# Probability transposes as 64-row halves in two PSUM banks, both heads together, in a block-causal attention and gated MLP kernel

## The chip, the cores and the metric

The kernel runs on one core of a Trainium2 chip. The core has a matrix engine, TensorE (PE in the profile; its weight loads stand apart as PEld), and three other compute engines: VectorE (DVE), ScalarE (ACT) and GpSimd (POOL). SyncE (SP) issues the DMAs here. Matmul results land in PSUM, which this kernel uses as eight banks of 512 fp32 columns for each of the 128 partitions. The metric is the device time of one execution in microseconds (us), as the median over runs; lower is better.

## The reference

Attention with a block-causal mask (blocks of 64), over 8 batches of 8 heads, 576 positions and 64 columns a head, then a gated MLP in which the gate mixes positions:

```python
scores = scale * np.matmul(q, k.transpose(0, 1, 3, 2))
mask = block_i >= block_j
scores = np.where(mask, scores, -1000000000.0)
scores = scores - np.max(scores, axis=-1, keepdims=True)
attn = np.exp(scores)
attn = attn / (np.sum(attn, axis=-1, keepdims=True) + 1e-09)
x = np.matmul(attn, v)            # heads side by side: (8, 576, 512)
...
h = np.maximum(x @ w_in, 0.0)     # 1024 columns
u, v = (h[..., :d_ff // 2], h[..., d_ff // 2:])
v_n = (v - mu) / np.sqrt(var + 1e-06)
v_s = np.einsum('ts,bsd->btd', w_spatial, v_n) + b_spatial[None, :, None]
return (u * v_s) @ w_out
```

The inputs are fp32, save the weights w_in and w_out, which come as 64-bit floats and are narrowed on the chip.

## The kernel before

**Tiling.** Heads go in pairs: 4 pairs a batch, 32 in all. The queries and keys of a pair lie on 128 partitions, 64 for each head. A pair has seven slots, `SLOTS`, each a tile of probabilities `p` of 128 query rows by up to 576 key columns: slots 0 and 1 hold query blocks 0 and 1 of the first and second head (128 + 256 columns), slots 2 and 3 block 2 (384 columns), slots 4 and 5 block 3 (512 columns), and slot 6 the last 64 queries of both heads, one head on each half of the partitions (576 columns).

**The steps of a slot.** `scores` (L265) and `scores_last` (L277) make the products on TensorE; after the first batch each is three products of a high and a low part. The score matmuls of L265 contract 64 rows, one head on each half of the array, and the profile shows them as 64*128. `exps` takes the negated maximum on DVE (L296, L305) and the exponential on ACT (L312). `norm` adds a small number and inverts the sum on DVE (L321, L324) and scales `p` on POOL (L326). `transposes` turns `p` so that keys lie on partitions (L352, L366): the tile of p is the loaded operand and the identity the moving one. The result is copied from PSUM (L354, L356, L361, L367) into `ptlo` (query blocks 0 and 1), `pthi` (blocks 2, 3 and the last queries) and `c4` (the last 64 keys). When all seven slots are there, `av` multiplies by the values (`avl` L396, `avh` L405) and `x_evac` (L382, L383) takes the result out in a high and a low part.

**PSUM.** Four banks serve the scores (`ps_s`), two the transposes and the `av` results together (`ps_t`), and two the MLP (`ps_m`). In `transposes` each slot takes one bank, slot 6 a second one for its last 64 keys.

**The MLP.** `moe` returns 29 groups for a finished batch, each some 8 to 24 matmuls in one bank: `mv` (L436, L447), `mu` (L505), `ms` (L528, L532, L533) and `mo` (L549). These are called expert matmuls below. They wait in `queue` and are dealt out over the 28 slots of the next batch.

**Order.** One loop runs over all slots, and in step n it emits, in this order: at slot 0 the scores of slots 0 to 3, the load of the next values and the background work that splits operands; `norm` of slot n-1; at slot 2 the scores of slots 4 and 5 and the `av` of the pair before; at slot 5 the last scores; `transposes` of slot n-2; about one MLP group; and `exps` of slot n. So on TensorE the transposes of slot 5 stand behind the scores of the next pair, those of slot 0 behind `av`, those of slot 3 behind `scores_last`, and the others between MLP groups. The compiler's scheduler may move single instructions from this order where it takes an operand to be late.

Of the kernel before, what the change touches and what calls it, by code (L numbers as in the profile page):

```python
# [10 lines left out]
F32 = mybir.dt.float32  # L11
# [6 lines left out]
P = 128  # L18
S = 576
# [9 lines left out]
SLOTS = [(0, 0, 1), (1, 0, 1), (0, 2, 2), (1, 2, 2), (0, 3, 3), (1, 3, 3), (2, 4, 4)]  # L29
NS = len(SLOTS)  # L30
# [6 lines left out]
def kernel(  # L37
# [10 lines left out]
    nc = tc.nc  # L48
# [8 lines left out]
    FULL = S // P  # L57

    const = ctx.enter_context(tc.tile_pool(name="const", bufs=1))
# [4 lines left out]
    pt_p = ctx.enter_context(tc.tile_pool(name="pt_p", bufs=1))  # L64
# [5 lines left out]
    ps_t = ctx.enter_context(tc.tile_pool(name="ps_t", bufs=2, space=PSUM))  # L70
# [5 lines left out]
    ident = const.tile([P, P], F32, name="ident")  # L76
# [21 lines left out]
    vs_b = const.tile([P, DH], F32R, name="vs_b")  # L98
    nc.gpsimd.memset(vs_b[64:97, :].bitcast(F32), 1.0)
    nc.gpsimd.memset(ws_b[64:97, :].bitcast(F32), 0.0)  # L100
    c4 = const.tile([P, P], F32, name="c4")
    nc.gpsimd.memset(c4[64:P, :], 0.0)

    staged = []

# [94 lines left out]
    def load_pair(b, pr):  # L200
        if b == 0 and pr % 2:
            raw = ff_p.tile([P, ND, S], F32, tag="u", name=f"raw_{b}_{pr}")
            raw = raw.rearrange("p c t -> p (c t)")[:, :KQ]
        else:
            raw = raw_p.tile([P, KQ], F32, tag="raw", name=f"raw_{b}_{pr}")
        if b == 0 and pr == 0:
            for cs in (slice(0, 256), slice(S, S + 256), slice(256, S), slice(S + 256, KQ)):
                nc.sync.dma_start(raw[:, cs], qk[b, pr, :, cs])
        else:
            nc.sync.dma_start(raw, qk[b, pr])  # L210
        raws[(b, pr)] = raw

    def prep_pair(b, pr):

        raw = raws.pop((b, pr))
        hi = hl_p.tile([P, KQ], F32R, tag="hi", name=f"hi_{b}_{pr}")
        lo = hl_p.tile([P, KQ], F32R, tag="lo", name=f"lo_{b}_{pr}")
        split_of[(b, pr)] = (hi, lo)
        for cs in (slice(0, S), slice(S, KQ)):
            nc.scalar.copy(hi[:, cs], raw[:, cs])  # L220
            yield
        for n, cs in enumerate((slice(S, Q8), slice(0, HT), slice(HT, S), slice(Q8, KQ))):
            (nc.vector if n == 0 else nc.gpsimd).tensor_tensor(  # L223
                out=lo[:, cs], in0=raw[:, cs], in1=hi[:, cs].bitcast(F32), op=ALU.subtract
            )
            yield
# [3 lines left out]
    def load_v(b, pr):  # L230
        vt = v_p.tile([P, FULL + 1, P], F32, tag="v", name=f"v_{b}_{pr}")
        nc.sync.dma_start(vt, v[b, pr])
        vts[(b, pr)] = vt
# [18 lines left out]
    def scores(b, pr, slots):  # L252

        parts = operands(b, pr)
        for i in slots:
            banks[(b, pr, i)] = s_bank(b, f"{b}_{pr}_{i}", slots[0] == 4)
        for i in slots[::2]:
            o = 0
            for t in range(SLOTS[i][1], SLOTS[i][2] + 1):
                n = P * (t + 1)  # L260
                qs = slice(S + t * P, S + (t + 1) * P)
                for m, (a, k) in enumerate(parts):
                    for hd in range(2):
                        js = slice(64 * hd, 64 * hd + 64)
                        nc.tensor.matmul(  # L265
                            banks[(b, pr, i + hd)][:, o:o + n], a[js, qs], k[js, :n],
                            start=(m == 0), stop=(m == len(parts) - 1),
                        )
                o += n
# [12 lines left out]
    ptiles = {}  # L282
# [50 lines left out]
    def pt_tiles(b, pr):  # L333
        if (b, pr) not in pts:
            lo = pt_p.tile([P, 2, 384], F32, tag="ptlo", name=f"ptlo_{b}_{pr}")
            hi = pt_p.tile([P, 2, 4, 320], F32, tag="pthi", name=f"pthi_{b}_{pr}")
            pts[(b, pr)] = (lo, hi)
        return pts[(b, pr)]

    def transposes(b, pr, i):  # L340
        hd, t0, t = SLOTS[i]
        pt = ptiles.pop((b, pr, i))[0]
        lo, hi = pt_tiles(b, pr)

        def bank(tag):
            return ps_t.tile([P, 512], F32, tag="t", name=f"t_{b}_{pr}_{tag}")

        bk = bank(i)
        n = 3 if t == 1 else min(t + 1, 4)

        for c in range(n):
            nc.tensor.transpose(bk[:, c * P:(c + 1) * P], pt[:, c * P:(c + 1) * P], ident)  # L352
        if t == 1:
            (nc.scalar.copy if b == 0 else nc.vector.tensor_copy)(lo[:, hd, :], bk[:, 0:384])  # L354
        elif hd < 2:
            nc.scalar.copy(  # L356
                hi[:, hd, 0:n, (t - 2) * P:(t - 1) * P],
                bk[:, :n * P].rearrange("p (c q) -> p c q", q=P),
            )
        else:  # L360
            nc.scalar.copy(  # L361
                hi[:, :, :, 256:320].rearrange("p h c q -> p c h q"),
                bk.rearrange("p (c h q) -> p c h q", c=4, h=2),
            )
            bk = bank(f"{i}c4")
            nc.tensor.transpose(bk[0:64, 0:P], pt[:, 4 * P:S], ident)  # L366
            nc.scalar.copy(c4[0:64, :], bk[0:64, 0:P])  # L367

    xts = {}
    tails = {}  # L370
# [8 lines left out]
    def x_evac(b, pr, av, q0, n):  # L379
        x = x_tiles(b, pr)  # L380
        qs = slice(q0, q0 + n)
        nc.scalar.copy(x[:, 0, qs], av[:, :n])  # L382
        nc.vector.tensor_tensor(  # L383
            out=x[:, 1, qs], in0=av[:, :n], in1=x[:, 0, qs].bitcast(F32), op=ALU.subtract
        )

    def av(b, pr):

        lo, hi = pts.pop((b, pr))
        vt = vts.pop((b, pr))  # L390
        al = ps_t.tile([P, 512], F32, tag="t", name=f"avl_{b}_{pr}")
        ah = ps_t.tile([P, 512], F32, tag="t", name=f"avh_{b}_{pr}")
        for c in range(2):
            for j in range(2):
                js = slice(64 * j, 64 * j + 64)
                nc.tensor.matmul(  # L396
                    al[js, c * P:256], vt[:, c, js],
                    lo[:, j, 0:256] if c == 0 else lo[:, j, 256:384],
                    start=(c == 0), stop=(c == 1),
                )  # L400
        for c in range(5):
            for j in range(2):
                js = slice(64 * j, 64 * j + 64)
                q0 = (0, 0, 0, 128, 256)[c]
                nc.tensor.matmul(  # L405
                    ah[js, q0:320], vt[:, c, js], hi[:, j, c, q0:] if c < 4 else c4[:, js],
                    start=(c == 0), stop=(c == 4),
                )
        x_evac(b, pr, al, 0, 256)
        x_evac(b, pr, ah, 256, 320)  # L410
        x = xts[(b, pr)]

        nc.gpsimd.tensor_scalar(
            out=tails[b][:, pr], in0=x[:, :, FULL * P:].bitcast(F32), scalar1=1.0, scalar2=1.0,
            op0=ALU.mult, op1=ALU.mult,
        )
# [166 lines left out]
    def spread(gen, n, first, last):  # L583
        background.append([gen, n / (last - first), first, 0.0])
# [22 lines left out]
    def at(n):  # L607

        g, i = divmod(n, NS)
        return (*pairs[g], i) if 0 <= g < len(pairs) else None  # L610

    for n in range(N + 2 * NS):
        g, i = divmod(n, NS)
        here = pairs[g] if g < len(pairs) else None
        if here and i == 0:
            scores(*here, (0, 1, 2, 3))
        if here and g + 1 < len(pairs):
            b, pr = pairs[g + 1]
            if i == 0:
                load_v(b, pr)  # L620
                if g + 1 >= NPAIR:
                    load_pair(b, pr)
            if n == 0:
                load_pair(0, 1)
            if i == LAST + 1 and g + 2 < NPAIR:
                load_pair(0, g + 2)
            if i == 1 and b > 0:
                spread(prep_pair(b, pr), 7, n, n + 4)
        step_background(n)
        if at(n - 1):  # L630
            norm(*at(n - 1))
        if i == RUN2:
            if here:
                scores(*here, (4, 5))
            if 0 < g <= len(pairs):
                av(*pairs[g - 1])
                if g % NPAIR == 0:
                    gs = moe(pairs[g - 1][0])
                    queue += gs
                    rate = len(gs) / (NPAIR * NS)  # L640
        if here and i == LAST:
            scores_last(*here)
        if n >= 2 and at(n - 2):
            transposes(*at(n - 2))
        credit += rate
        while credit >= 1.0 and queue:
            queue.pop(0)()
            credit -= 1.0
        if at(n):
            exps(*at(n))  # L650
# [47 lines left out]
```

## Time and profile before

| what | value |
|---|---|
| time, median of 3 runs | 767.68 us (765.17 to 773.61) |
| span of the profiled execution, first to last instruction | 763.8 us |
| busy TensorE | 740.3 us (97%), 5508 matmuls |
| busy weight loads | 636.0 us (83%) |
| busy DVE, ACT, POOL | 471.9, 436.1 and 318.4 us |
| mean granted TensorE clock | 0.996 |

The span is given for the profiled execution alone; its time beside the span is not recorded. A row of the timeline reads: start in us from the span's start, length in us from the first instruction's start to the last one's end, engine, line, operation, output <- inputs, tile of the array (rows*columns), moving operand, how many instructions are merged; in brackets the engine's idle time before and what ended it. A row of a group has, behind the bar, busy us and mean ns of one instruction, then the idle time of the engine before such instructions. A matmul's length holds its way through the array, so matmuls overlap; the step from one start to the next tells what one costs in a stream. In a row of the waits stand the total in us, the number of waits and, last, the longest.

### The profile page before, as it was taken

To read this page: it belongs to the slowest core of one execution; us is meant where nothing else is said; L and a number is where in the kernel's file an instruction comes from. 1 tells how busy PE (TensorE), PEld (TensorE's weight loads), DVE (VectorE), ACT (ScalarE), POOL (GpSimd) and SP (SyncE) were. 2 spreads that over 40 slices of the span, in tenths; PEclk is the share of its full clock that TensorE was granted. 3 is DMA by queue.
4 is the path that set the end of the run, shared out by engine and by line. 5 is a ranking of instruction groups with operands and counts; after the bars stand their busy time and mean duration, and the time that the engine had idled before them with its cause. 6 is when DMAs were issued, how large, how long until landed. Compare 5 with 4: busy or idle time off the path is not lost.

```text
span 763.8 us, 15854 instructions
## 1 busy us (share of the span) xinstructions
PE 740.3 (97%) x5508; PEld 636.0 (83%) x5508; DVE 471.9 (62%) x1743; ACT 436.1 (57%) x1236; POOL 318.4 (42%) x480
## 2 busy tenths in 40 slices
PE   8998889999999999999999999999999999999998
PEld 5556678987998878898888888898789987889898
DVE  6985984548745577547764577455874557742641
ACT  6885665656665556654655656564666555653232
POOL 4786465423444334442344423542344433431011
PEclk9999999999999999999999999999999999999999
DMA  6453231221122111221012211122112211000001
GB/s 215 151 170 103 84 98 33 75 82 34 52 69 72 42 51 51 69 71 58 18 51 82 78 38 50 30 71 84 33 52 73 67 42 51 18 33 32 1 9 55
DMA packets 21411, 48.63 MB, mean 64 GB/s; under 512 B 2386, under 2 KB 11090, under 8 KB 21332
## 3 DMA queue, kind: packets, MB, share of 16 engines
q1 hardware_dynamic: 21332, 47.63, 19.7%
q8 instruction: 44, 0.72, 0.4%
q14 instruction: 35, 0.29, 0.1%
HBM read 38.18 MB, written 9.44 MB: 62 GB/s over the span
## 4 chain that ended last, share of the span: by engine, by line
PE 81%; DVE 8%; ACT 5%; POOL 2%; issue 2%; DMA 1%; SPq 0%; ACTq 0%; DVEq 0%; POOLq 0%
PE mo L549 14%; PE ms L528 13%; PE mu L505 10%; PE t L352 10%; PE mv L436 10%; PE s L265 7%; PE avh L405 6%; PE s L277 3%; PE avl L396 2%; ACT p L312 2%; PE mv L447 1%; DVE st L457 1%; POOL p L326 1%; PE ms L533 1%; PE ms L532 1%
## 5 line engine op out<-in xcount | busy, mean ns | idle before, releaser
L326 POOL TENSOR_SCALAR p<-p,ssum 128x128 f32<-128x128 f32 (+4 forms) x288 | 177.9, 630 | 209.9 <-DVE ssum L324 173.9
L312 ACT ACTIVATE p<-p,nmax 128x128 f32<-128x128 f32 (+4 forms) x288 | 166.9, 581 | 59.6 <-DVE nmax L296 47.3
L296 DVE CUSTOM_DVE_ANT_0 p<-s,mask 128x128 f32<-128x128 f32 (+3 forms) x256 | 115.4, 484 | 62.8 <-PE s L265 62.7
L352 PE MATMUL t<-ident,p 128*128 128x128 f32 x768 | 124.6, 278 | 10.5 <-POOL p L326 7.2
L505 PE MATMUL mu<-x,wi_hi 128*128 128x288 f32 x512 | 116.5, 304 | 0.6 <-DVE vr L453 0.5
L352 PEld LDWEIGHTS t<-ident,p 128*128 128x128 f32 x768 | 90.6, 141 | 27.8 <-POOL p L326 12.3
L223 POOL TENSOR_TENSOR lo<-raw,hi 128x288 fp32r<-128x288 f32 (+1 forms) x84 | 66.9, 815 | 80.8 <-ACT hi L220 80.7
L436 PE MATMUL mv<-wi_hi,x 128*128 128x512 f32 x256 | 87.0, 401 | 0.0
L505 PEld LDWEIGHTS mu<-x,wi_hi 128*128 128x128 f32 x512 | 85.5, 188 | 1.4 <-DVE vr L453 0.7
L356 ACT COPY pthi<-t 128x512 f32<-128x512 f32 (+1 forms) x128 | 67.0, 525 | 29.1 <-PE t L352 28.8
L537 POOL TENSOR_TENSOR gl<-u,gh 128x288 fp32r<-128x288 f32 x48 | 38.7, 807 | 99.6 <-ACT gh L536 99.6
L528 PE MATMUL ms<-ws_hi,vh 128*128 128x288 f32 x256 | 80.0, 313 | 0.0
L535 DVE TENSOR_TENSOR u<-ms,u 128x288 f32<-128x288 f32 x64 | 29.3, 458 | 78.1 <-PE ms L533 78.0
L528 PE MATMUL ms<-ws_hi,vl 128*128 128x288 f32 x256 | 75.4, 294 | 0.0
L528 PE MATMUL ms<-ws_lo,vh 128*128 128x288 f32 x256 | 75.3, 294 | 0.0
L549 PE MATMUL mo<-gh,wo_hi 128*128 128x288 f32 x256 | 74.7, 315 | 0.0
L549 PE MATMUL mo<-gh,wo_lo 128*128 128x288 f32 x256 | 70.0, 295 | 0.0
L505 PE MATMUL mu<-x,wi_lo 128*128 128x288 f32 x256 | 69.7, 295 | 0.0
L536 ACT CAST gh<-u 128x288 fp32r<-128x288 f32 x64 | 27.8, 434 | 71.8 <-DVE u L535 71.8
L321 DVE TENSOR_SCALAR ssum<-ssum 128x1 f32<-128x1 f32 (+1 forms) x224 | 37.2, 166 | 50.8 <-ACT p L312 50.8
L405 PE MATMUL avh<-pthi,v 128*64 128x320 f32 (+1 forms) x512 | 67.9, 407 | 0.0
L405 PEld LDWEIGHTS avh<-pthi,v 128*64 128x64 f32 x512 | 36.0, 138 | 24.2 <-issue 0.3
(114 smaller groups left out, 1648.4 us busy)
## 6 DMA issues: line engine op xcount, KB each, us to landing
raw<-qk SPq DMA_DIRECT2D x31, 608.0 KB, 3.9
v<-v SPq DMA_DIRECT2D x32, 320.0 KB, 3.0
outT<-o SPq DMA_DIRECT2D x64, 144.0 KB, 1.8
rwi<-w_in SPq DMA_DIRECT2D x8, 512.0 KB, 4.6
rwo<-w_out SPq DMA_DIRECT2D x4, 512.0 KB, 3.7
rws<-w_spT SPq DMA_DIRECT2D x4, 288.0 KB, 2.7
rwt<-w_spT SPq DMA_DIRECT2D x2, 144.0 KB, 2.8
raw<-qk SPq DMA_DIRECT2D x2, 128.0 KB, 2.3
```

Source lines behind the costliest of these rows:

```text
L223: (nc.vector if n == 0 else nc.gpsimd).tensor_tensor(out=lo[:, cs], in0=raw[:, cs], in1=hi[:, cs].bitcast(F32), op=ALU.subtract)
L265: nc.tensor.matmul(banks[(b, pr, i + hd)][:, o:o + n], a[js, qs], k[js, :n], start=(m == 0), stop=(m == len(parts) - 1),)
L296: nc.vector.tensor_tensor_reduce(out=pt[:, o:o + n], in0=bk[:, o:o + n], in1=mask[:, 512 - n:], scale=-0.125, scalar=BIG, op0=ALU.add, op1 ...
L312: nc.scalar.activation(pt[:, o:o + n], pt[:, o:o + n], AF.Exp, bias=mx, scale=-1.0, accum_out=ssum[:, r:r + 1],)
L326: nc.gpsimd.tensor_scalar(out=pt[:, o:o + n], in0=pt[:, o:o + n], scalar1=ssum[:, 2 + r:3 + r], scalar2=1.0, op0=ALU.mult, op1=ALU.mult,)
L352: nc.tensor.transpose(bk[:, c * P:(c + 1) * P], pt[:, c * P:(c + 1) * P], ident)
L356: nc.scalar.copy(hi[:, hd, 0:n, (t - 2) * P:(t - 1) * P], bk[:, :n * P].rearrange("p (c q) -> p c q", q=P),)
L405: nc.tensor.matmul(ah[js, q0:320], vt[:, c, js], hi[:, j, c, q0:] if c < 4 else c4[:, js], start=(c == 0), stop=(c == 4),)
L436: nc.tensor.matmul(ps, xs[k][:, j, cs], w[:, k, DH:], start=(n == 0), stop=(n == 3 * NC - 1),)
L505: nc.tensor.matmul(ps[:, :HT], w[:, k, ds], xs[k][:, j, zs], start=(n == 0), stop=(n == 3 * NC - 1),)
L528: nc.tensor.matmul(ps[:, :HT], a[:, ds], w[:, k, zs], start=(n == 0), stop=False)
L549: nc.tensor.matmul(ps[:, :HT], w[:, k, es], a[:, k, :], start=(n == 0), stop=(n == 3 * ND - 1),)
```

## The change

Each 128-row transpose becomes two of 64 rows: the halves z = 0 and 1 of the partitions of `p` are transposed with the matching 64x64 corner of the identity into two banks, one for each half, 64 columns each. `transposes` takes both heads of a query block at once: slots 0 and 1, 2 and 3, 4 and 5, each in the step in which the odd slot was transposed before; slot 6 alone, where it was. The 25 transposes of a head pair become 50. Each bank is then copied at once for both heads, so the copies stay eight a pair. The last key chunk of slot 6 is no longer the 64 keys behind 512 in a tile of their own, but the last 128 keys, of which the first 64 meet zero rows: v is laid out on the host with 64 zero rows and then the last 64. `c4` and its memset go, and `pthi` has five chunks in place of four.

```diff
-    c4 = const.tile([P, P], F32, name="c4")
-    nc.gpsimd.memset(c4[64:P, :], 0.0)
...
-            hi = pt_p.tile([P, 2, 4, 320], F32, tag="pthi", name=f"pthi_{b}_{pr}")
+            hi = pt_p.tile([P, 2, 5, 320], F32, tag="pthi", name=f"pthi_{b}_{pr}")
...
-    def transposes(b, pr, i):
-        hd, t0, t = SLOTS[i]
-        pt = ptiles.pop((b, pr, i))[0]
+    def transposes(b, pr, slots):
+        t = SLOTS[slots[0]][2]
+        src = [ptiles.pop((b, pr, i))[0] for i in slots]
         lo, hi = pt_tiles(b, pr)
-        def bank(tag):
-            return ps_t.tile([P, 512], F32, tag="t", name=f"t_{b}_{pr}_{tag}")
-
-        bk = bank(i)
-        n = 3 if t == 1 else min(t + 1, 4)
-
-        for c in range(n):
-            nc.tensor.transpose(bk[:, c * P:(c + 1) * P], pt[:, c * P:(c + 1) * P], ident)
-        if t == 1:
-            (nc.scalar.copy if b == 0 else nc.vector.tensor_copy)(lo[:, hd, :], bk[:, 0:384])
-        elif hd < 2:
-            nc.scalar.copy(
-                hi[:, hd, 0:n, (t - 2) * P:(t - 1) * P],
-                bk[:, :n * P].rearrange("p (c q) -> p c q", q=P),
-            )
+        halves = [
+            ps_t.tile([P, 512], F32, tag="t", name=f"t_{b}_{pr}_{slots[0]}_{z}")
+            for z in range(2)
+        ]
+        if len(slots) == 1:
+            cols = [slice(c * P, (c + 1) * P) for c in range(FULL)] + [slice(S - P, S)]
         else:
-            nc.scalar.copy(
-                hi[:, :, :, 256:320].rearrange("p h c q -> p c h q"),
-                bk.rearrange("p (c h q) -> p c h q", c=4, h=2),
-            )
-            bk = bank(f"{i}c4")
-            nc.tensor.transpose(bk[0:64, 0:P], pt[:, 4 * P:S], ident)
-            nc.scalar.copy(c4[0:64, :], bk[0:64, 0:P])
+            cols = [slice(c * P, (c + 1) * P) for c in range(3 if t == 1 else t + 1)]
+        n = len(cols)
+        for h, pt in enumerate(src):
+            for c, cs in enumerate(cols):
+                for z in range(2):
+                    zs = slice(64 * z, 64 * z + 64)
+                    o = (h * n + c) * 64
+                    nc.tensor.transpose(halves[z][:, o:o + 64], pt[zs, cs], ident[zs, zs])
+        for z in range(2):
+            if len(slots) == 1:
+                nc.scalar.copy(
+                    hi[:, z, :, 256:320],
+                    halves[z][:, :n * 64].rearrange("p (c q) -> p c q", q=64),
+                )
+                continue
+            bk = halves[z][:, :2 * n * 64].rearrange("p (h c q) -> p h c q", h=2, q=64)
+            if t == 1:
+                (nc.scalar.copy if b == 0 else nc.vector.tensor_copy)(
+                    lo.rearrange("p h (c q) -> p h c q", q=P)[:, :, :, 64 * z:64 * z + 64], bk
+                )
+            else:
+                q0 = (t - 2) * P + 64 * z
+                nc.scalar.copy(hi[:, :, 0:n, q0:q0 + 64], bk)
...
-                    ah[js, q0:320], vt[:, c, js], hi[:, j, c, q0:] if c < 4 else c4[:, js],
+                    ah[js, q0:320], vt[:, c, js], hi[:, j, c, q0:],
...
-            transposes(*at(n - 2))
+            b, pr, j = at(n - 2)
+            if j % 2 or j == NS - 1:
+                transposes(b, pr, (j,) if j == NS - 1 else (j - 1, j))
...
-    vp[:, :, :S] = v
+    vp[:, :, :512] = v[:, :, :512]
+    vp[:, :, 576:] = v[:, :, 512:]
```

## The prediction

> **What bounds the kernel now.** I read the slices of the page first, then busy time by window, the chain that ended last, groups of instructions by shape, and last the timeline of TensorE (PE, and PEld for its weight loads) around a transpose.
>
> ```profile
> 0.00:100.00 100.00, 86.82 (x503) 57.95 (x504) 79.73 (x292) 69.15 (x190) 64.49 (x87) 0.97 0.45 146
> 300.00:400.00 100.00, 99.18 (x772) 87.20 (x769) 60.70 (x229) 56.27 (x161) 40.78 (x64) 1.00 0.18 54
> PE 81%; DVE 8%; ACT 5%; POOL 2%; issue 2%; DMA 1%; SPq 0%; ACTq 0%; DVEq 0%; POOLq 0%
> 158.21 3.19 PE mo L549 x24
> 248.84 3.19 PE mo L549 x24
> ```
>
> The first two rows are windows: length, busy PE, PEld, DVE, ACT, POOL, clock, DMA. In the first 100 us PE idles 13%; in a later window 99.2% is covered and no other engine passes 61%. The last two rows are pieces of the chain one batch apart: 90.63 us for four head pairs, 22.7 us for one. From 100 to about 700 us PE sets the pace, so I count what the change adds to or takes from PE's stream in one head pair, times 27 (600 / 22.7 = 26.5, and a part of the pair before).
>
> **A transpose as it is.** Three between two expert matmuls:
>
> ```profile
> 304.25 0.30 PE L533 MATMUL ms<-ws_b,vs_b 97*128 97x288 f32 x1
> 304.38 0.49 PE L352 MATMUL t<-ident,p 128*128 128x128 f32 x3
> 304.63 0.38 PE L528 MATMUL ms<-ws_hi,vh 128*128 128x288 f32 x1
> 304.85 0.29 PE L528 MATMUL ms<-ws_lo,vh 128*128 128x288 f32 x1
> ```
>
> From 304.25 to 304.85 is 0.60; two matmuls at their usual step of 0.13 leave 0.33, so 0.11 for each transpose and nothing for entering or leaving. What makes up the 0.11, the moving identity or the load of p?
>
> ```profile
> L352 PE MATMUL t<-ident,p 128*128 128x128 f32 x768 | 124.6, 278 | 10.5 <-POOL p L326 7.2 <-DVE ssum L324 1.6 <-DVE x L383 1.0
> L405 PE MATMUL avh<-pthi,v 128*64 128x320 f32 x384 | 57.5, 434 | 0.0
> L405 PE MATMUL avh<-c,v 128*64 128x64 f32 x128 | 9.1, 220 | 0.0
> L352 PEld LDWEIGHTS t<-ident,p 128*128 128x128 f32 x768 | 90.6, 141 | 27.8 <-POOL p L326 12.3 <-issue 9.4 <-PE s L265 1.5
> L366 PEld LDWEIGHTS t_6c<-ident,p 128*64 128x64 f32 x32 | 3.5, 110 | 8.1 <-ACT pthi L356 5.6 <-ACT pthi L361 1.5 <-ACT hi L220 0.8
> 293.82 0.66 PE L352 MATMUL t<-ident,p 128*128 128x128 f32 x4
> 301.94 0.28 PE L405 MATMUL avh<-c,v 128*64 128x64 f32 x4
> ```
>
> In the fp32 matmuls 256 more columns cost 434 - 220 = 214 ns, 0.84 ns a column. The transpose, with 128 columns, lasts 278, on that line (220 + 54 = 274). So its identity streams 128 x 0.84 = 107 ns: that is the 0.11. Its load is shorter: 64 columns fewer save 31 ns, so 128 stream in about 62. The row at 293.82 shows it directly: after a pause four transposes take 0.66, less the last one's 0.27 is 0.39 for three steps; two are 0.11, and the first, in which matmul one waits on its own load, is 0.17, 0.06 more. The row at 301.94 is two pairs of 64-column matmuls: 0.28 less one's 0.22 is 0.06 from pair to pair.
>
> **The change, part by part.** Per head pair 25 transposes (3, 3, 3, 3, 4, 4, 4 and the 64-column one) become 25 pairs of 64-row halves. Moving columns fall from 128 to 64 (54 ns); the load stays at 128 columns (about 0.058 until its matmul may start). If the two halves of a pair run together, I get 0.058 a pair instead of 0.109; ends 0.056 and 0.109. They do for scores, which are 64-row pairs too:
>
> ```profile
> 291.77 0.69 PE L505 MATMUL mu<-x,wi_hi 128*128 128x288 f32 x4
> 292.39 0.18 PEld L265 LDWEIGHTS s<-hi 64*128 64x128 f32 x2 [0.17 <-issue]
> 292.39 0.33 PE L265 MATMUL s<-hi 64*128 64x128 f32 x2
> 292.56 0.27 PE L265 MATMUL s<-lo,hi 64*128 64x128 f32 x2
> 292.67 0.28 PE L265 MATMUL s<-hi,lo 64*128 64x128 f32 x2
> 293.54 0.35 PE L265 MATMUL s<-hi,lo 64*128 64x384 f32 x2
> 294.24 0.38 PE L505 MATMUL mu<-x,wi_hi 128*128 128x288 f32 x1
> PEld s L265 <- issue: 9.7, 52, 0.4
> ```
>
> Both heads lie within one row. But the entry is dear. The last expert matmul starts at 292.17 (291.77 + 0.69 - 0.29); the first score shows at 292.39 and is 0.05 longer than the next of its shape, so it runs from 292.45: 0.28 after, not 0.13. The load stood idle 0.17 with nothing to wait for; the waits list 52 such gaps between 100 and 700 us, two a head pair. Leaving costs too. One lone score matmul stands inside an output group:
>
> ```profile
> 152.51 0.29 PE L549 MATMUL mo<-gh,wo_lo 128*128 128x288 f32 x1
> 152.73 0.32 PE L265 MATMUL s<-hi 64*128 64x128 f32 x1
> 153.01 0.40 PE L549 MATMUL mo<-gh,wo_hi 128*128 128x288 f32 x1
> 153.25 0.30 PE L549 MATMUL mo<-gh,wo_lo 128*128 128x288 f32 x1
> ```
>
> It runs from 152.78; the expert matmul behind it is 0.11 too long, so from 153.12: 0.34 to leave. The half transpose streams 0.05 less: 0.29. Leaving scores for transposes was quicker by some 0.03, so I take 0.27, with 0.26 to 0.29 as ends. A group of n pairs between expert matmuls thus costs 0.28 + 0.058(n - 1) + 0.27 - 0.13 = 0.36 + 0.058n, where n transposes now cost 0.109n.
>
> ```profile
> 302.15 0.55 PE L352 MATMUL t<-ident,p 128*128 128x128 f32 x3
> 302.45 0.38 PE L528 MATMUL ms<-ws_hi,vh 128*128 128x288 f32 x1
> ```
>
> - Slots 0 and 1: slot 0 now stands behind the attention product, whose last pair starts at 302.00, and expert work runs from 302.54 (302.45 + 0.09): 0.54. Without it, 0.27. Slot 1 costs 0.33. Now 0.60, then 0.36 + 6 x 0.058 = 0.71: +0.11.
> - Slots 2 and 3: 0.66 now, 0.71 then: +0.05.
> - Slots 4 and 5: slot 4 costs 0.44; slot 5 stands behind scores (last at 293.55) and expert work runs from 294.32: 0.77. Together 1.21. Then they follow scores without a switch: 0.165 + 7 x 0.058 + 0.27 = 0.84: -0.37.
> - Slot 6: 5 x 0.109 = 0.55 now, 0.36 + 5 x 0.058 = 0.65 then: +0.10.
>
> The sum is -0.11 us a head pair, -3.0 us over 27: six new switches nearly eat what the shorter stream gives.
>
> **Waits.** A merged group needs both banks empty, so slot 6 waits for both copies of slots 4 and 5; its waiting load holds all expert matmuls behind it.
>
> ```profile
> 295.92 0.60 PE L352 MATMUL t<-ident,p 128*128 128x128 f32 x4
> 295.06 0.57 ACT L356 COPY pthi<-t 128x512 f32<-128x512 f32 x1
> 182.67 0.60 PE L352 MATMUL t<-ident,p 128*128 128x128 f32 x4
> 183.30 0.56 ACT L356 COPY pthi<-t 128x512 f32<-128x512 f32 x1
> 183.92 0.30 PE L366 MATMUL t_6c<-ident,p 128*64 128x128 f32 x1 [0.66 <-ACT pthi L356]
> 183.98 0.48 PE L436 MATMUL mv<-wi_hi,x 128*128 128x512 f32 x1
> PE t L352 <- DVE x L383: 1.0, 6, 0.2
> ```
>
> Usually slot 5's copy ends at 295.63, 0.29 before slot 6 starts; a second copy behind it ends about 0.5 later: 0.15 of waiting, twice a batch. In the second head pair of a batch ACT takes the copy only at 183.30 and the small transpose waits already; with two copies slot 6 starts at 184.4 and expert work at 185.0, not 184.06: 0.93, of which 0.10 is counted. Per batch 0.83 + 2 x 0.15 = 1.13, times 6.75 = +7.6 us; ends 0 (ACT may take both copies before the exponentials) and 15 (twice that). Slot 0 no longer waits for DVE behind the attention product: -1.0.
>
> **Edits at nothing.** The copies keep their count and elements (eight a head pair; the last 512 and 128 columns become two of 320) and ACT is at 56% there. The even slot's p is held one step longer; seven buffers cover it, else the exponentials would stall. Without c4 one POOL memset goes; the larger hi tile and the moved rows of v change no transfer's size. In the first 100 us PE waits for others: 0, ends -2 and +2.
>
> Sum: -3.0 + 7.6 - 1.0 = +3.6 on a span of 763.8. The span says nothing of what lies around it; the median of the runs, 767.68, is 3.9 above it. Forecast 767.7 + 3.6 = 771, which is within 1%, about what a measurement of this kernel can tell from no change.
>
> **Rivals.**
> - Slower, because the pair step stays at 0.109: the two halves' loads run one behind the other (2 x 0.058), or four instructions a pair come no faster. The score pairs at 292.56 and 292.67 step by 0.11, which speaks for it; but they carry 128 moving columns. It costs 25 x 0.051 x 27 = +34: 805. It decides from a step of 0.066 on. The Trainium skill, page "TensorE: Matmul & The Clock Gate", section LDWEIGHTS, has the load go by columns alone, at 1.2 columns a ns whatever the rows: by it 107 ns for 128 columns (an estimate), so this rival and 805 us. The trace disagrees: 0.06 from load to matmul, 31 ns for 64 columns.
> - Slower, because the instruction order splits merged groups, as that lone score matmul was split off: one more switch in and out, the lone one took 0.74 from 152.51 to 153.25, where two expert steps alone take 0.26; with the pair's own 0.06 off that is some 0.4 a head pair, +11: 782.
> - Faster, because transposes pay less for the switch: the 97-row matmul at 304.25 and the 64-column load change shape at no cost. With half of the 0.36 in the three groups that are new between expert matmuls (0.54 a head pair) it is -15: 756; with none of it, 742. A quarter off is enough for a gain of 1%. The 52 gaps at scores speak against it. The Trainium skill, page "TensorEngine Tiling (Array Packing)", section Key Properties, says that a change of tiling mode drains TensorE; by that the whole price stands and it is 771, and the gap of 0.17 agrees.
>
> **How the numbers follow.** Forecast and its neighbours within 1%: 0.52. Step stays: 0.18. Split groups or twice the copy waits: 0.16. Cheaper switch: 0.14. So faster 0.14, same 0.52, slower 0.34. The terms' ends give -3.0 with 1.3 for the step and 2 for leaving, copies 0 to 15, the start 2: about 759 to 782. Reaching to the split groups above and half the switch price below, and leaving out most of the 0.18 and what lies beyond half the switch price: 756 to 788.
>
> **What would show it.** Row-tiled transposes should last about 0.22, pairs step by 0.056 to 0.06; loads should idle some 0.15 at three more entries a head pair; the waits of transposes for the copies should grow from a few us to about ten; PE should stay at 98% or more from 100 us on. A step near 0.11, or entries without a gap, makes the forecast wrong.

## The result, and the profile after

The changed kernel takes 788.99 us (median of 4 runs, 788.02 to 789.47), the kernel before 766.42 (764.17 to 773.61) beside it: a ratio of 1.0263, 95% interval 1.0211 to 1.0316. It is slower. The forecast of 771 was too low: 788.99 lies 1 us above the range's upper end of 788, and the ratio on the forecast's own base (1.0263 x 767.68 = 787.9) lies just inside it. The profiled execution took 789.47 us, with a span of 787.7.

First the windows, with the same columns as before (length, busy PE, PEld, DVE, ACT, POOL, clock, DMA), and then the page's chain by engine:

```profile
0.00:100.00 100.00, 82.54 (x646) 61.36 (x647) 84.14 (x299) 70.37 (x194) 64.66 (x89) 0.90 0.47 148
300.00:400.00 100.00, 95.69 (x847) 81.39 (x844) 59.58 (x233) 57.79 (x169) 40.55 (x65) 1.00 0.18 57
```

```profile
PE 76%; DVE 11%; ACT 7%; issue 3%; DMA 2%; SPq 0%; POOL 0%; ACTq 0%; DVEq 0%; POOLq 0%
```

From 300 to 400 us PE was covered for 99.18 us before, and is for 95.69 now. A head pair of 22.7 us so holds about 0.8 us more in which PE stands still. The start is not where the time went: the first expert matmul behind slot 6 of the sixth head pair starts at 114.18 us, and started at 115.12 before. The loss accrues afterwards, a head pair at a time. The waits between 105 and 720 us (total, number, longest) name it, and the groups by shape say what the transposes themselves became:

```profile
PE t L356 <- ACT pthi L371: 22.0, 26, 2.3
...
PEld t L356 <- POOL p L324: 19.7, 20, 2.5
...
PEld t L356 <- issue: 17.4, 59, 1.3
```

```profile
L356 PE MATMUL t<-ident,p 64*128 64x64 f32 x1304 | 69.4, 229 | 24.5 <-ACT pthi L371 22.0
...
L371 ACT COPY pthi<-t 128x512 f32<-128x512 f32 x52 | 27.1, 570 | 0.0
```

Transposes wait 22.0 us for copies out of PSUM, 26 times; the window holds 26 head pairs (1304 halves, 50 a pair), so once in each, 0.85 on the mean. In the same window of the kernel before, this was all of the kind:

```profile
PE t_6c L366 <- ACT pthi L356: 3.9, 6, 0.7
```

One of the 26, on PE, on ACT, and slot 6's scaling on POOL (start, length, engine, line):

```profile
205.79 0.35 PE L263 MATMUL s<-hi,lo 64*128 64x384 f32 x2
205.96 0.67 PE L356 MATMUL t<-ident,p 64*128 64x64 f32 x16
206.56 0.40 PE L509 MATMUL mu<-x,wi_hi 128*128 128x288 f32 x1
...
209.10 0.91 PE L356 MATMUL t<-ident,p 64*128 64x64 f32 x10 [0.68 <-ACT pthi L371]
209.95 0.40 PE L532 MATMUL ms<-ws_hi,vh 128*128 128x288 f32 x1
```

```profile
206.03 0.40 ACT L310 ACTIVATE p<-p,nmax 128x128 f32<-128x128 f32 x1 [0.75 <-DVE nmax L294]
...
206.43 0.49 ACT L310 ACTIVATE p<-p,nmax 128x256 f32<-128x256 f32 x1
...
206.92 0.39 ACT L310 ACTIVATE p<-p,nmax 128x128 f32<-128x128 f32 x1
...
207.31 0.49 ACT L310 ACTIVATE p<-p,nmax 128x256 f32<-128x256 f32 x1
...
207.80 0.60 ACT L310 ACTIVATE p<-p,nmax 128x384 f32<-128x384 f32 x1
...
208.40 1.04 ACT L371 COPY pthi<-t 128x512 f32<-128x512 f32 x2
```

```profile
205.01 1.17 POOL L324 TENSOR_SCALAR p<-p,ssum 128x576 f32<-128x576 f32 x1 [0.98 <-ACT vs_a L495]
```

The transposes of slots 4 and 5 are through at 206.63. ACT takes their two copies only at 208.40, behind five exponentials: those of slots 0 and 1 of the next head pair (128 + 256 columns each) and that of slot 2 (384). Slot 6 needs both banks; its group starts late and takes 0.85 us (209.10 to 209.95) for five pairs, and the expert matmuls behind it stand. The list puts 20 gaps of the loads down to POOL, but POOL had scaled slot 6's p by 206.18, so here it is the copies that the load waited for as well. Before, slot 5's copy stood behind three of these exponentials, and the other bank had been emptied long since:

```profile
293.78 0.40 ACT L312 ACTIVATE p<-p,nmax 128x128 f32<-128x128 f32 x1 [0.87 <-DVE nmax L296]
...
294.18 0.49 ACT L312 ACTIVATE p<-p,nmax 128x256 f32<-128x256 f32 x1
...
294.68 0.39 ACT L312 ACTIVATE p<-p,nmax 128x128 f32<-128x128 f32 x1
...
295.06 0.57 ACT L356 COPY pthi<-t 128x512 f32<-128x512 f32 x1
295.53 0.51 ACT L312 ACTIVATE p<-p,nmax 128x256 f32<-128x256 f32 x1
...
296.03 0.61 ACT L312 ACTIVATE p<-p,nmax 128x384 f32<-128x384 f32 x1
...
296.63 0.61 ACT L312 ACTIVATE p<-p,nmax 128x384 f32<-128x384 f32 x1
```

The pairs themselves are as foreseen: in the row at 205.96, eight pairs take 0.67 less the last half's 0.22, so seven steps of 0.064.

### The profile page after: what moved, and what is told of

It is laid out like the page before. It is cut to its first block, busy times and chain, and to the rows that moved or that the text cites. A ratio compares the mean times of both kernels' runs of the same rounds, so it can differ in the third digit from the quotient of the medians.

```text
span 787.7 us, 17379 instructions
## 1 busy us (share of the span) xinstructions
PE 742.0 (94%) x6308; PEld 627.5 (80%) x6308; DVE 475.1 (60%) x1743; ACT 435.7 (55%) x1236; POOL 318.7 (40%) x479
## 4 chain that ended last, share of the span: by engine, by line
PE 76%; DVE 11%; ACT 7%; issue 3%; DMA 2%; SPq 0%; POOL 0%; ACTq 0%; DVEq 0%; POOLq 0%
PE ms L532 14%; PE mo L553 13%; PE mv L440 11%; PE mu L509 9%; PE avh L409 7%; PE t L356 6%; PE s L263 6%; DVE p L294 4%; ACT pthi L371 3%; PE avl L400 3%; PE s L275 3%; ACT p L310 2%; PE mv L451 2%; PE ms L537 1%; PE ms L536 1%
## 5 line engine op out<-in xcount | busy, mean ns | idle before, releaser
L324 POOL TENSOR_SCALAR p<-p,ssum 128x128 f32<-128x128 f32 (+4 forms) x288 | 175.0, 618 | 234.8 <-DVE ssum L322 132.1
L356 PE MATMUL t<-ident,p 64*128 64x64 f32 x1600 | 94.6, 235 | 39.6 <-ACT pthi L371 25.1
L356 PEld LDWEIGHTS t<-ident,p 64*128 64x128 f32 x1600 | 76.4, 143 | 68.0 <-issue 28.7
L221 POOL TENSOR_TENSOR lo<-raw,hi 128x288 fp32r<-128x288 f32 (+1 forms) x84 | 70.2, 860 | 75.7 <-ACT hi L218 75.2
L409 PE MATMUL avh<-pthi,v 128*64 128x320 f32 (+2 forms) x640 | 71.2, 369 | 0.0
L319 DVE TENSOR_SCALAR ssum<-ssum 128x1 f32<-128x1 f32 (+1 forms) x224 | 35.4, 159 | 58.9 <-ACT p L310 58.8
L409 PEld LDWEIGHTS avh<-pthi,v 128*64 128x64 f32 x640 | 44.9, 137 | 25.3
L371 ACT COPY pthi<-t 128x512 f32<-128x512 f32 (+1 forms) x128 | 62.0, 521 | 4.3 <-PE t L356 4.1
```

What stands on the lines that cost most here:

```text
L221: (nc.vector if n == 0 else nc.gpsimd).tensor_tensor(out=lo[:, cs], in0=raw[:, cs], in1=hi[:, cs].bitcast(F32), op=ALU.subtract)
L324: nc.gpsimd.tensor_scalar(out=pt[:, o:o + n], in0=pt[:, o:o + n], scalar1=ssum[:, 2 + r:3 + r], scalar2=1.0, op0=ALU.mult, op1=ALU.mult,)
L356: nc.tensor.transpose(halves[z][:, o:o + 64], pt[zs, cs], ident[zs, zs])
L371: nc.scalar.copy(hi[:, :, 0:n, q0:q0 + 64], bk)
L409: nc.tensor.matmul(ah[js, q0:320], vt[:, c, js], hi[:, j, c, q0:], start=(c == 0), stop=(c == 4),)
```

## The experiments

**Theory A**: the pairs are worth what the prediction counted, and the loss is the order on ACT: the copies of slots 4 and 5 behind exponentials that nobody needs yet. **Rival B**: the halves or the switches of tiling cost more than counted, and PE's waits only show up where there is slack. **Rival C**: merging two heads into one group does it, whatever the size of the transposes.

| kernel | median us (runs) | ratio to before, 95% interval |
|---|---|---|
| the change | 788.99 (4) | 1.0263, 1.0211 to 1.0316 |
| copies_first | 760.99 (6) | 0.9911, 0.9876 to 0.9946 |
| full_rows_copies_first | 764.68 (10) | 0.9959, 0.9933 to 0.9984 |
| halves_apart | 790.48 (4) | 1.0276, 1.0216 to 1.0336 |
| three_switches | 795.03 (4) | 1.0347, 1.0291 to 1.0403 |
| before_copy_first | 764.43 (10) | 0.9958, 0.9926 to 0.9990 |
| full_merged | 766.85 (10) | 0.9984, 0.9954 to 1.0013 |
| halves_behind_scores | 756.16 (4) | 0.9861, 0.9814 to 0.9908 |
| apart_copies_first | 785.21 (4) | 1.0236, 1.0192 to 1.0281 |

The first four after the change ran on one chip beside the kernel before at 767.49 us (15 runs), the last four on another beside it at 766.71 (19 runs).

**copies_first.** The changed kernel with one order added: slot 1's exponentials follow the two copies of slots 4 and 5 of the pair before.

```diff
+    behind = [None]
...
+            if i == 1 and behind[0] is not None:
+                es.enter_context(tc.issue_after(behind[0]))
             for r, (o, n, mx) in enumerate(runs):
...
-                nc.scalar.copy(hi[:, :, 0:n, q0:q0 + 64], bk)
+                last = nc.scalar.copy(hi[:, :, 0:n, q0:q0 + 64], bk)
+        if slots[0] == 4:
+            behind[0] = last.ins
```

> The changed kernel, with ACT's two copies of slots 4 and 5 put ahead of the exponentials of the next pair's slot 1. Theory A (slot 6 waits for those copies): the 1.05 to 1.4 us that its group waits in each of some 28 head pairs goes, 29 us, so 789 falls to about 760. Theory B (the six new switches of array tiling in a head pair are the loss, and the wait only shows there): at most a few us go, above 780.

It takes 760.99 us, 28 less than the change and less than the kernel before. Its window, its waits between 105 and 700 us, one pass from the scores to the group behind slot 6, and the two copies on ACT in that pass:

```profile
300.00:400.00 100.00, 99.16 (x884) 85.39 (x882) 61.05 (x226) 57.52 (x163) 42.49 (x64) 1.00 0.17 52
```

```profile
PEld t L360 <- issue: 18.5, 80, 0.9
PE t L360 <- ACT pthi L375: 5.8, 13, 0.8
```

```profile
198.57 0.65 PE L360 MATMUL t<-ident,p 64*128 64x64 f32 x16
199.16 0.40 PE L515 MATMUL mu<-x,wi_hi 128*128 128x288 f32 x1
...
200.95 0.53 PE L360 MATMUL t<-ident,p 64*128 64x64 f32 x10
201.40 0.40 PE L538 MATMUL ms<-ws_hi,vh 128*128 128x288 f32 x1
```

```profile
199.53 1.05 ACT L375 COPY pthi<-t 128x512 f32<-128x512 f32 x2
```

The copies now start 0.96 behind the first transpose (198.57 to 199.53). PE is back at 99.16, the wait falls to 5.8 us, from 21.3 in the same window of the change, and slot 6's group takes 0.45 (200.95 to 201.40) instead of 0.85. What is left of the wait lies in the second head pair of each batch, where ACT comes late to the copies. The transposes, switches and copies are the same, so the late copies were the loss, and B cannot be.

**full_rows_copies_first.** The same order and the same merged groups, but whole 128-row transposes, one bank for each head.

```diff
-                for z in range(2):
-                    zs = slice(64 * z, 64 * z + 64)
-                    o = (h * n + c) * 64
-                    nc.tensor.transpose(halves[z][:, o:o + 64], pt[zs, cs], ident[zs, zs])
+                bk, o = (halves[h], c) if len(slots) == 2 else (halves[c // 4], c % 4)
+                nc.tensor.transpose(bk[:, o * P:(o + 1) * P], pt[:, cs], ident)
```

> As copies_first, but with whole 128-row transposes in place of the halves: heads still merged, one bank a head, and no new switches. Theory A: halves and switches about cancel, so it equals copies_first within 5 us, about 758 to 764. Theory B: it is 20 us or more faster than copies_first.

764.68 us, on the same chip as copies_first: at equal order the halves, with their three switches more, are worth 3.7 us against whole rows.

**full_merged.** The edit above made to the changed kernel, with no order added.

> The changed kernel with whole 128-row transposes, one bank a head, both heads of a query block together; no order forced on ACT. It tells which part of the change made the copies late. If merging alone does it (both copies of slots 4 and 5 wait behind exponentials of the next pair), slot 6 waits about 0.8 us a head pair more than in full_rows_copies_first (764.7) and the time is 785 to 795. If the scheduler puts the copies behind slot 1's first exponential only, they end 0.4 us sooner or more and the time is 766 to 772: then it was the halves, which fill both banks only at the end of the group, that made them late.

766.85 us: within 0.5% of the kernel before. So merging alone does not cost the time, and C falls. The waits between 105 and 700 us, and one pass on PE and on ACT, say why:

```profile
PE t L354 <- ACT pthi L370: 6.0, 6, 1.0
```

```profile
198.97 1.09 PE L354 MATMUL t<-ident,p 128*128 128x128 f32 x8
...
201.50 0.71 PE L354 MATMUL t<-ident,p 128*128 128x128 f32 x5
```

```profile
200.19 0.38 ACT L310 ACTIVATE p<-p,nmax 128x128 f32<-128x128 f32 x1
...
200.57 1.04 ACT L370 COPY pthi<-t 128x512 f32<-128x512 f32 x2
```

Here the scheduler has put three exponentials ahead of the copies (the third is slot 1's first, at 200.19), not five. Counted from the first transpose of slots 4 and 5, the copies start 1.60 us later; in the change they start 2.44 later (205.96 to 208.40). And slot 6 comes 2.53 us behind the first transpose of slots 4 and 5, when one copy is done and the other nearly; in the change it would have come 2.4 behind (198.57 to 200.95 in copies_first). Merging costs the time only where the order on ACT makes both copies late, as it did with the halves. Why the scheduler orders halves and whole rows differently no run shows: the kernel's code puts the copies in the same place.

**before_copy_first.** The kernel before with the same order: slot 5's copy ahead of slot 1's exponentials.

```diff
-            nc.scalar.copy(
+            last = nc.scalar.copy(
                 hi[:, hd, 0:n, (t - 2) * P:(t - 1) * P],
                 bk[:, :n * P].rearrange("p (c q) -> p c q", q=P),
             )
+            if i == 5:
+                behind[0] = last.ins
```

> The kernel before with one thing added: slot 5's copy is put ahead of slot 1's exponentials of the next head pair on ACT. The kernel before waits for that copy at slot 6's small transpose in the second head pair of each batch (waits of PE for it 3.9 us, of the load 5.3 us, six times each). If the late copy alone cost that, the time falls by 4 to 5 us, from 767.5 to about 763. If pushing the exponentials back costs as much in another place, it stays at 767 or above. Whatever it gains is the part of the gain of copies_first (28 us) that has nothing to do with halves.

0.42% faster (interval 0.10 to 0.74), some 3.2 us; 4 to 5 were expected. Of the 28 us that the order gives the changed kernel, about 3 were to be had without the change. Against this kernel, copies_first is 0.47% (0.9958 to 0.9911), 3.6 us, faster.

**halves_apart** and **apart_copies_first.** All first halves of a group ahead of all second halves, in the changed kernel and in copies_first.

```diff
-        for h, pt in enumerate(src):
-            for c, cs in enumerate(cols):
-                for z in range(2):
-                    zs = slice(64 * z, 64 * z + 64)
+        for z in range(2):
+            zs = slice(64 * z, 64 * z + 64)
+            for h, pt in enumerate(src):
+                for c, cs in enumerate(cols):
```

> The changed kernel, with all first halves of a group ahead of all second halves, so that no two neighbours use different rows of the array. If the halves of a pair run together in the changed kernel: 25 more steps of 0.06 us in a head pair, +40 us, about 829. If they run one behind the other there too: no change, 789.

> copies_first (761.0) with all first halves ahead of all second halves in each group, so that a pair's two halves don't stand next to each other. If halves run two at a time only as neighbours, groups of 6, 8 and 5 pairs last as long as in halves_apart (0.69 for 0.52, 0.89 for 0.59, about 0.78 us a head pair) with nothing left that hides it: 761 + 21 = 782. If TensorE starts the second halves early enough for the order not to matter, the time stays at 761 to 765.

halves_apart, at 790.48 us, cannot be told from the change. Its groups are longer, but its wait for the copies is 5.5 us between 105 and 700 us where the change has 21.3, so one hid the other, and the run settled nothing by itself. With the copies first there is nothing left to hide behind: 785.21 against 760.99, by the ratios 3.25% or 25 us, 0.92 a head pair. Three groups of apart_copies_first, and below them one of copies_first with its neighbours:

```profile
200.79 0.77 PE L360 MATMUL t<-ident,p 64*128 64x64 f32 x12
...
206.21 0.96 PE L360 MATMUL t<-ident,p 64*128 64x64 f32 x16
...
208.89 0.64 PE L360 MATMUL t<-ident,p 64*128 64x64 f32 x10
```

```profile
193.12 0.29 PE L275 MATMUL s<-hi,lo 128*128 128x288 f32 x1
193.34 0.59 PE L360 MATMUL t<-ident,p 64*128 64x64 f32 x12
193.86 0.40 PE L515 MATMUL mu<-x,wi_hi 128*128 128x288 f32 x1
194.10 0.29 PE L515 MATMUL mu<-x,wi_lo 128*128 128x288 f32 x1
```

Sixteen halves take 0.96 apart and 0.65 as neighbours, twelve 0.77 and 0.59, ten 0.64 and 0.53: 0.31 + 2 x 0.18 + 0.11 = 0.78 of the 0.92. By these lengths, half of the array stands idle for part of the time when a half's partner is not next in line.

**three_switches.** The kernel before with one 64-row transpose added behind the whole-row ones of slots 1, 2 and 3; its result is not read.

```diff
+        if i in (1, 2, 3):
+            nc.tensor.transpose(bk[:, 384:448], pt[0:64, 0:P], ident[0:64, 0:64])
```

> The kernel before, with one more 64-row transpose of 64 columns behind the whole ones of slots 1, 2 and 3, its result unused: three more excursions to row tiles in a head pair. If each costs the 0.36 to 0.42 us of the prediction: 27 x 3 x 0.36 to 0.42 = 29 to 34 us, 796 to 800. If transposes pay no switch: 3 x 0.06 x 27 = 5 us, 771.

3.47% (2.91 to 4.03) is 27 us (22 to 31); over 81 excursions (three in each of 27 head pairs) 0.33 us for one, the transpose itself included, where 0.36 to 0.42 was expected. Its waits between 105 and 700 us show the entry, and one pass the whole price:

```profile
PEld t L354 <- issue: 12.4, 74, 0.2
```

```profile
315.54 0.30 PE L535 MATMUL ms<-ws_b,vs_b 97*128 97x288 f32 x1
315.67 0.49 PE L352 MATMUL t<-ident,p 128*128 128x128 f32 x3
316.09 0.27 PE L354 MATMUL t<-ident,p 64*128 64x64 f32 x1
...
316.53 0.30 PE L530 MATMUL ms<-ws_lo,vh 128*128 128x288 f32 x1
```

74 loads stand idle 0.17 each without a releaser, as they did ahead of the scores. From 315.54 to 316.53 is 0.99, where the same stretch without the excursion took 0.60 in the kernel before (304.25 to 304.85): 0.39.

**halves_behind_scores.** Halves only where TensorE is in 64-row tiling anyhow: slots 4 and 5, together behind the scores. Slots 0 to 3 and 6 stay whole, one head at a time; the copies go first; slot 6 uses the change's layout of the last keys.

```diff
+            b, pr, j = at(n - 2)
+            if j == 5:
+                halves_of(b, pr, (4, 5))
+            elif j != 4:
+                transposes(b, pr, j)
```

> Halves only where TensorE is in 64-row tiling already: slots 4 and 5, together behind the scores; slots 0 to 3 and 6 as before, whole rows; copies of slots 4 and 5 ahead of the exponentials. By the prediction's terms slots 4 and 5 give -0.37 us a head pair, -10 us over 27, with no new switch anywhere, and the order gives 4 to 5 us: 767.5 - 14.5 = 753. If the switch out of the scores was cheaper before than the prediction had it, or the merged group costs a wait for the copies in each head pair, it comes out no better than copies_first: 761 or above.

756.16 us, ratio 0.9861 (0.9814 to 0.9908): the lowest of all, 5 us under copies_first, though on another chip; by the ratios it is 3.8 us, and their intervals overlap. One pass, and its waits from 105 to 700 us:

```profile
308.25 0.34 PE L263 MATMUL s<-hi,lo 64*128 64x384 f32 x2
308.43 0.66 PE L360 MATMUL t<-ident,p 64*128 64x64 f32 x16
309.02 0.40 PE L588 MATMUL mo<-gh,wo_hi 128*128 128x288 f32 x1
```

```profile
PE t L391 <- ACT pthi L375: 5.2, 6, 0.9
...
PEld t L360 <- issue: 0.3, 2, 0.2
```

The transposes follow the scores at their own step (308.43 less 308.25 is 0.18), with no gap of their loads (L360 here): two idle entries, 0.3 us, not 80. Against before_copy_first it gains 0.97%, 7.4 us or 0.28 a head pair, where 0.37 was expected (the two intervals leave some 4 us either way). In six head pairs slot 6 still waits for two copies, 5.2 us in all where before_copy_first waits 1.6; these 3.6 us would make up what is missing.

## Where the prediction held and where it failed

**The pair step, 0.058 for 0.109.** Right in the main. The change shows 0.064, copies_first 0.061 ((0.65 - 0.22) / 7 in the row at 198.57): a little above the 0.056 to 0.06 that was to show it, but under the 0.066 from which the rival decides. A half lasts 0.22 as foreseen. The rival at 805 us is out. The Trainium skill, page "TensorE: Matmul & The Clock Gate", section LDWEIGHTS, by whose rule of columns alone that rival would have come, is not borne out here: eight pairs of loads of 128 columns go by in 0.65 with their matmuls, one pair every 0.061, not every 0.107 (an estimate from the page's rate).

**The price of the switch.** Right. The loads idle three times a head pair ahead of halves (80 entries in copies_first). The group of six pairs at 193.34 lies between matmuls that start 0.98 apart (193.12 to 194.10); less two steps of 0.13 it costs 0.72, and the group formula gives 0.71. One excursion costs 0.39 in the trace of three_switches, where the formula gives 0.36 + 0.058; its times give 0.33 (0.27 to 0.38), so by the times alone a price a quarter lower could not be ruled out. The rows and the gain that stays small rule out the rival of the cheaper switch. Its sentence that a quarter off is enough for a gain of 1% does not come out of its own numbers: 1% under 767.7 is 760, 11 us under 771, and that is some 0.4 of the 29 us that the whole price in the three groups is worth. The Trainium skill, page "TensorEngine Tiling (Array Packing)", section Key Properties, says that a change of mode drains TensorE, without a price; this is one, and the run agrees with the rule.

**The sum of the slots, -3.0 us, and slot 0's wait for DVE, -1.0.** Right within what the runs can tell: 3.6 us between before_copy_first and copies_first, where the order on ACT is alike (the two intervals leave some 3.6 either way), and 3.7 between full_rows_copies_first and copies_first on one chip. That it is so close to 4.0 is in part luck: copies_first still waits 5.8 us for copies, and before_copy_first 1.6. The part of slots 4 and 5 (-0.37 a head pair) measured -0.28 with, and about -0.4 without, the waits that came with it.

**The start, 0, and PE at 98% or more.** The first held: at the sixth head pair the change is 0.9 us ahead, within the ends of 2. The second did not: 95.69.

**The copy waits, +7.6 us: the step that failed.** The mechanism was named and placed: slot 6 waits for both copies of slots 4 and 5, and the expert matmuls stand behind it. Its size was not. By the ratios, the late copies cost 27 us (1.0263 less 0.9911), of which the kernel before already had 3: some 24 in place of 7.6 (the intervals leave about 5 either way), and beyond the upper end of 15. I took 0.83 for one head pair of a batch, 0.15 for two, and for the fourth nothing, without a reason. The 0.15 came from slot 5's copy, which ended 0.29 before slot 6 started; a second copy was to run straight behind it. That kept ACT's order of before, in which one copy stood behind three exponentials. But ACT's order is the scheduler's and not the code's. In the change both copies stand behind five (in the second head pair of a batch behind three that start late themselves: copies at 185.73, slot 6 at 186.44), and PE waits in every head pair: 22.0 us in 26 waits, 0.85 each. My range priced the case that ACT takes both copies ahead of the exponentials (0), and not the opposite one, all exponentials that can be ready ahead of both copies. The rows for that were at hand in the kernel before: from 293.78 to 296.63 ACT takes five such exponentials and, from 295.06 to 295.53, one copy, so the five take 2.4 us, while slot 6 started 2.1 us behind slot 5's first transpose (293.82 to 295.92). Put behind all five, both copies lie almost wholly in PE's way: 1.04 us less what one bank lets start.

**The other rivals.** The case "split groups or twice the copy waits", given 0.16, came nearest, by its second half and for more than twice; no group was split.

**The sum, mended.** -3.6 for the slots and about +24 for the copies are +20 us, or a ratio of 1.027. That this meets the measured 1.0263 is no test, for both terms are differences of ratios that add up to it; it says how the 20 us divide. The trace bears out the larger part on its own: between 105 and 700 us the waits for copies fall by 15.5 us from the change to copies_first.

## What to carry to other kernels

When a change fills two buffers together where it filled them one after the other, look at where the emptying engine will stand at that moment, and price the wait with every instruction that can be ready placed ahead of the copies; then bind that order yourself rather than leave it to the scheduler. Put 64-row work next to 64-row work: here eight pairs behind the scores gave no less than all 25 pairs with three more switches (7.4 and 3.6 us, each with some 4 either way). And a measurement of a part beside a free-moving wait says little (halves_apart): first take the wait out.

## What the hardware showed beside this

In halves_apart six first halves stand ahead of six second halves in the program, and yet the starts of one group of twelve come close together in its middle: 202.102, .217, .280, .287, .342, .398, .405, .459, .466, .521, .584 and .648. I had thought of one stream after the other, twelve steps of 0.06 or 0.7 in all, or of no loss. It is 0.55 from the first start to the last, where the same group as neighbours has 0.37 (0.59 less 0.22). The records don't say which half of the array an instruction is on, but the starts part into two streams of six with one rhythm each, first a step of 0.115 or 0.118 and then steps of 0.055 to 0.064: .102, .217, .280, .342, .398, .459 and .287, .405, .466, .521, .584, .648. The first matmul of each of these streams lasts 0.27, the other ten 0.22, which fits this reading. Read so, the second half of the array begins 7 ns after the third transpose of the first, ahead of three that stand before it in the program; and a half alone steps as slowly as a pair. The Trainium skill, page "TensorE: Matmul & The Clock Gate", section The mechanism, has matmuls start strictly in the program's order; these starts do not fit that, by this reading.
